# A linear-attention layer with an MLP: another way to spread u, first weights in halves, and other chunks for transposes by DMA

## The chip, the cores and the metric

The kernel runs on one core of a Trainium2 chip. A core has TensorE (PE, matrix products; its weight loads are shown as PEld), VectorE (DVE), ScalarE (ACT), GpSimd (POOL) and SyncE (SP), which here issues nearly all transfers, and 16 DMA engines that carry them. The metric is device time in microseconds, the median of several runs. A profile is one more execution, taken by the hardware profiler.

## What is computed

For each of 4 x 8 heads (batch, head), with 768 steps and width 48, a state of 48 x 48 is carried along; its output of all heads, 384 values a token, goes through an MLP with 2048 hidden values and a leaky ReLU. All inputs are float32.

```python
for t in range(S):
    cur = einsum('bhd,bhe->bhde', u[None] * kt, vt)
    y[:, :, t] = einsum('bhd,bhde->bhe', rt, state + cur)
    state = wt[:, :, :, None] * state + einsum('bhd,bhe->bhde', kt, vt)
x = y.transpose(0, 2, 1, 3).reshape(B * S, H * D)      # 3072 x 384
h = x @ w_in                                           # 3072 x 2048
out = maximum(0.01 * h, h) @ w_out                     # 3072 x 384
```

## The kernel before

The 3072 tokens are 24 chunks of 128 tokens, six for each of the four batch entries. Within a chunk the recurrence is written as matrix products: the logarithm of w is taken (ACT) and summed along time on TensorE (L475, L677), two exponentials of the sums scale r and k (`rk`, L370), `rk` is transposed (`rkT`), scores are formed (L584, L818), masked (`m`, L596, L748) and multiplied with v (`vb`) and with the carried state (`sb`, L612, L619, L784, L789). The term with u is made apart by GpSimd and VectorE: k times u (L400), times r (L404), summed (L408), times v (L412), then added to the output `y`. The output is transposed into `xT`, the MLP's input.

Chunks 0 to 3 are treated as two pairs (`pair`): one load brings 256 tokens, and both chunks go through together. Chunks 4 to 23 go through `single`, each with four loads of 192 KB (w, k, r, v), and `run` forms the scores of one chunk, or of two in one step where the first is in `MERGED`. Each transpose can be done in two ways. On TensorE, `rk` takes eight transposes and two copies out of PSUM (L381, then L386 or L388), an output takes three and one copy (L429, then L434 or L436). By DMA it is one transfer issued by SP (L724 for `rk` of the chunks in `RK_DMA`, L803 for outputs of those in `Y_DMA`).

The MLP runs in blocks of one or two chunks (`blocks`). In a block, 16 parts of the hidden width are formed (up-projection, L860, into `hp`; activation L875 into `g`) and then added up for each chunk in four groups (down-projection, L887), copied out of PSUM (L898, L900) and stored (L904). The weights come in eight loads, four quarters of `w_in` (L313) and four of `w_out` (L318). Each goes through one of ten SBUF buffers of pool `in`, which the loads of chunks use as well, and is cast to bf16 in two halves (L336, L338, L340). An up-projection depends on both casts of the quarter it reads.

Nothing of the order is fixed by the compiler. Every piece of work is a step with a guessed duration for each engine that can do it, a priority, dependences and buffers; class `Plan` runs the steps through an event queue, lets each free engine take the ready step of lowest priority number, and emits the instructions in that order. Each engine works through its own instructions in this order and waits where data are missing. A step with a transfer carries a triple (`wire` time, size, latency). Attention steps of chunk n have priorities around 10 n, the MLP from 1000 on; a store has 5. `AHEAD` keeps the loads of chunk n from being planned before the first sums of chunk n - 8, `LEAD` keeps attention from running more than seven chunks ahead of the MLP. Until `WARM_UNTIL` (24 us of planned time), planned idle time of TensorE is filled with products of zeros (L922), one for each 0.08 us.

u is loaded as one row (L350) and spread over 128 partitions by a float32 product with a column of ones (`ones_f`, L358), then copied to `ub` (L364). The constants at which the planner starts are `BEGIN` (PE 1.1, DVE 3.8 us).

Of the kernel before, what the change touches and what calls it, by code (L numbers as in the profile page):

```python
# [8 lines left out]
F32 = mybir.dt.float32  # L9
# [13 lines left out]
class Plan:  # L23
# [18 lines left out]
    def order(self, pools):  # L42
# [30 lines left out]
        while events:  # L73
# [13 lines left out]
            for e in self.ENGINES:  # L87
# [39 lines left out]
                if wire is None:  # L127
                    self.done[i] = now + d + self.SEEN[e]
                    if self.slack_from <= pri < 1000:
                        self.done[i] += self.slack  # L130
                else:
                    wire, size, lat = wire
# [21 lines left out]

LOAD = (1.05, 64, 1.5)
BOTH = (1.47, 64, 1.6)
WEIGHT = (2.2, 24, 2.6)
STORE = (0.6, 8, 1.5)
ROWS = (0.6, 8, 1.5)
TRK = (1.75, 64, 1.8)  # L160
TY = (0.65, 24, 1.8)


@with_exitstack
def kernel(
# [88 lines left out]
    with tc.manual_schedule():  # L254
# [52 lines left out]

        def weight_steps(q, which, pri):
            st = Buf("in")

            def load(e):
                if which == 0:
                    nc.sync.dma_start(  # L313
                        out=st.t[:].rearrange("p (t f) -> p t f", t=KT),
                        in_=w_in_v[:, :, q * 512 : (q + 1) * 512],
                    )
                else:
                    nc.sync.dma_start(  # L318
                        out=st.t[:].rearrange("p (t f) -> p t f", t=JQ),
                        in_=w_out_v[:, q * JQ : (q + 1) * JQ, :],  # L320
                    )

            ld = step({"SP": 0.5}, load, pri, takes=[st], wire=WEIGHT)
            made = []
            for half in (0, 1):
                def cast(e, half=half):
                    if which == 0:
                        f0 = half * 256
                        o = w_in_b[:, :, q * 512 + f0 : q * 512 + f0 + 256]
                        i = st.t[:].rearrange("p (t f) -> p t f", t=KT)[:, :, f0 : f0 + 256]  # L330
                    else:
                        n = JQ // 2
                        o = w_out_b[:, q * JQ + half * n : q * JQ + (half + 1) * n, :]
                        i = st.t[:].rearrange("p (t f) -> p t f", t=JQ)[:, half * n : (half + 1) * n, :]
                    if e == "POOL":
                        nc.gpsimd.tensor_copy(out=o, in_=i)  # L336
                    elif e == "DVE":
                        nc.vector.tensor_copy(out=o, in_=i)  # L338
                    else:
                        nc.scalar.copy(out=o, in_=i)  # L340
                made.append(step(
                    {"DVE": 1.0 if which == 0 else 0.66, "ACT": 0.83, "POOL": 1.0}, cast, pri + 1, deps=[ld], reads=[st]))
            (win_s if which == 0 else wout_s).append(made)

# [11 lines left out]
        s_u = step(  # L356
            {"PE": 1.4},
            lambda e: nc.tensor.matmul(  # L358
                u_ps.t[:, 0:DM], lhsT=ones_f[:], rhs=u_row.t[0:1, :], start=True, stop=True, skip_group_check=True),
            -20, deps=[u_raw], reads=[u_row], takes=[u_ps])  # L360

# [285 lines left out]
        def single(n):  # L647
# [11 lines left out]
            for i, src in enumerate((w, k, r, v)):  # L659
                def load(e, src=src, i=i):  # L660
                    nc.sync.dma_start(out=part(i)(), in_=src[b, :, t0 : t0 + L, :].rearrange("h p d -> p h d"))
# [56 lines left out]
            if n not in RK_DMA:  # L718
                s_T = [transposes(P0, rk, a, s_d, rkT, lambda a=a: rkT.t[:, a * NP : (a + 1) * NP, :])
                       for a, s_d in ((0, s_r), (1, s_k))]  # L720
            else:
                s_T = [step(
                    {"SP": 0.6},
                    lambda e: nc.sync.dma_start_transpose(  # L724
                        out=rkT.t[:], in_=rk.t[:].rearrange("p a h d -> p (a h d)")),
                    P0, deps=[s_r, s_k], reads=[rk], takes=[rkT], wire=TRK)]
# [71 lines left out]
            if n not in Y_DMA:  # L798
                xt_steps[n] = [to_xt(P0, y, yp, s_ye, lambda: xT[:, :, col : col + L])]
            else:  # L800
                xt_steps[n] = [step(
                    {"SP": 0.6},
                    lambda e: nc.sync.dma_start_transpose(  # L803
                        out=xT[:, :, col : col + L], in_=y.t[:].rearrange("p h d -> p (h d)")),
                    P0 + 1, deps=[s_ye], reads=[y], wire=TY)]

# [23 lines left out]
        for n in range(NCH):  # L830
            for q, which in WEIGHTS_AT.get(n, []):
                weight_steps(q, which, n * 10 - 8)
            if n < done_to:
# [12 lines left out]
        for nb, size in enumerate(blocks):  # L846
# [33 lines left out]
            for ch in chs:  # L880
# [3 lines left out]
                for q in range(4):  # L884
                    def down(e, op=op, g=g, q=q, off=off):
# [70 lines left out]
```

## Time and profile before

| | |
|---|---|
| median of 3 runs | 183.1 us (182.97 to 184.17) |
| profiled execution | 185.71 us, its span 184.0 us |
| granted TensorE clock | 0.999 |
| busy: DVE, ACT, POOL | 114.0, 114.7, 98.9 us |
| DMA: moved, mean rate | 34.48 MB, 187 GB/s |
| DMA: time of packets, share of 16 engines' span | 88.5% |
| transposes by DMA: `xT`, `rkT` | 14 and 11, 3.7 and 4.0 us from issue to landing |
| loads of a chunk | 3.8 to 4.2 us from issue to landing |

Rows of the profile name the line of the kernel, the engine, the operation and the tiles (out <- in), with buffer numbers left out; xN counts instructions. In rows in order of time, the first number is the start and the second the length in microseconds, and a bracket gives the engine's idle time before it and what ended it. Rows with SPq are issues by SP: their length is the issuing, not the transfer. The chain of waits is followed back from the last instruction, at each step to what came last; its rows give start, length, engine and line. Rows by stretch give, behind the stretch and its length, busy time and number of instructions of PE, PEld, DVE, ACT and POOL, then the granted clock, the DMA share and GB/s. Ends of matmuls are modelled, so single matmuls are shown longer than the pace at which they follow one another.

### The profile page before, as it was taken

To read this page: it belongs to the slowest core of one execution; us is meant where nothing else is said; L and a number is where in the kernel's file an instruction comes from. 1 tells how busy PE (TensorE), PEld (TensorE's weight loads), DVE (VectorE), ACT (ScalarE), POOL (GpSimd) and SP (SyncE) were. 2 spreads that over 40 slices of the span, in tenths; PEclk is the share of its full clock that TensorE was granted. 3 is DMA by queue.
4 is the path that set the end of the run, shared out by engine and by line. 5 is a ranking of instruction groups with operands and counts; after the bars stand their busy time and mean duration, and the time that the engine had idled before them with its cause. 6 is when DMAs were issued, how large, how long until landed. Compare 5 with 4: busy or idle time off the path is not lost.

```text
span 184.0 us, 5300 instructions
## 1 busy us (share of the span) xinstructions
PE 176.9 (96%) x2091; PEld 133.8 (73%) x2091; DVE 114.0 (62%) x231; ACT 114.7 (62%) x251; POOL 98.9 (54%) x140
## 2 busy tenths in 40 slices
PE   7999999999999999999998999999999999999991
PEld 5676787777877888777685687776686686777750
DVE  4388864298898769695975487595383486521102
ACT  2566879685886886957384676574566663454510
POOL 6788610665978689764664549546347555000000
PEclk9999999999999999999999999999999999999999
DMA  5999999899997999899799998999699995520112
GB/s 143 261 261 369 382 376 329 155 224 213 185 225 137 212 178 223 147 222 185 134 180 160 216 178 179 219 139 223 146 231 203 167 242 93 121 64 4 43 43 86
DMA packets 116154, 34.48 MB, mean 187 GB/s; under 512 B 109473, under 2 KB 114594, under 8 KB 116130
## 3 DMA queue, kind: packets, MB, share of 16 engines
q1 hardware_dynamic: 116128, 34.16, 88.5%
q8 instruction: 16, 0.26, 0.7%
q14 instruction: 8, 0.07, 0.1%
q10 hardware_dynamic: 2, 0.00, 0.0%
HBM read 25.17 MB, written 4.72 MB: 162 GB/s over the span
## 4 chain that ended last, share of the span: by engine, by line
PE 80%; DMA 9%; DVE 3%; issue 2%; ACT 2%; SPq 1%; POOL 1%; DVEq 0%; ACTq 0%; POOLq 0%
PE ps L860 30%; PE ps L887 28%; DMA in<-in_r_dram 5%; PE ps L922 3%; PE ps L818 3%; PE ps L381 3%; DMA xT<-y 2%; DMA in<-in_v_dram 2%; PE ps L475 2%; PE ps L789 2%; PE ps L677 1%; PE ps L758 1%; PE ps L612 1%; DVE rk L370 1%; PE ps L784 1%
## 5 line engine op out<-in xcount | busy, mean ns | idle before, releaser
L860 PE MATMUL ps<-xT,w_in_b 128*128 128x256 bf16 (+1 forms) x672 | 74.2, 257 | 0.2
L887 PE MATMUL ps<-w_out_b,g 128*128 128x384 bf16 x384 | 73.9, 326 | 0.0
L875 ACT ACTIVATE g<-ps 128x512 bf16<-128x512 f32 x96 | 56.2, 597 | 27.7 <-PE ps L860 26.8
L860 PEld LDWEIGHTS <-w_in_b 128*128 128x128 bf16 x672 | 56.3, 98 | 10.0 <-issue 0.5
L887 PEld LDWEIGHTS <-g 128*128 128x128 bf16 x384 | 35.5, 98 | 17.5
L400 POOL TENSOR_TENSOR ru<-in,ub 128x384 f32<-128x384 f32 x24 | 23.9, 999 | 21.3 <-DMA in<-in_k_dram 18.0
L370 DVE TENSOR_TENSOR rk<-in,ps 128x384 bf16<-128x384 f32 x48 | 24.9, 549 | 13.0 <-DMA in<-in_r_dram 5.0
L748 DVE TENSOR_TENSOR m<-ps,maskb 128x512 bf16<-128x512 f32 x40 | 25.2, 683 | 6.6 <-PE ps L818 6.5
L404 POOL TENSOR_TENSOR ru<-ru,in 128x384 f32<-128x384 f32 x24 | 23.9, 999 | 4.2 <-DMA in<-in_r_dram 3.7
L898 DVE COPY o<-ps 128x384 f32<-128x384 f32 x12 | 6.7, 558 | 19.0 <-PE ps L887 18.8
L412 POOL TENSOR_TENSOR vs<-in,dg 128x384 f32<-128x384 f32 x20 | 16.6, 830 | 3.3 <-DVE dg L408 3.1
L735 POOL TENSOR_TENSOR sb<-s,a 128x384 bf16<-128x384 f32 x18 | 14.9, 829 | 4.4 <-ACT a L698 4.4
L420 POOL CAST vb<-in 128x384 bf16<-128x384 f32 x24 | 12.0, 505 | 9.8 <-DMA in<-in_v_dram 9.0
L689 DVE TENSOR_TENSOR ci<-ps,lw 128x384 f32<-128x384 f32 x20 | 11.1, 556 | 8.0 <-PE ps L680 3.2
L408 DVE TENSOR_REDUCE dg<-ru 128x8 f32<-128x384 f32 x24 | 13.1, 548 | 4.2 <-POOL ru L404 3.9
L671 ACT ACTIVATE lw<-in 128x384 bf16<-128x384 f32 x20 | 10.4, 522 | 5.4 <-DMA in<-in_w_dram 5.3
L443 DVE TENSOR_TENSOR y<-ps,vs 128x384 bf16<-128x384 f32 x20 | 11.1, 553 | 2.7 <-PE ps L789 2.2
L388 ACT COPY rkT<-ps 128x512 bf16<-128x512 bf16 x17 | 9.8, 586 | 3.5 <-PE ps L381 3.3
L698 ACT ACTIVATE a<-ps 64x4 f32<-64x4 f32 x36 | 6.1, 168 | 9.5 <-DVE ci L689 6.4
L703 ACT ACTIVATE ps<-ps 128x384 f32<-128x384 f32 x20 | 9.6, 482 | 2.0 <-DVE ci L689 1.9
L381 PE MATMUL ps<-ident,rk 128*128 128x128 bf16 x104 | 10.0, 223 | 0.2
L707 ACT ACTIVATE ps<-ci 128x384 f32<-128x384 f32 x20 | 9.8, 490 | 0.0
(87 smaller groups left out, 172.8 us busy)
## 6 DMA issues: line engine op xcount, KB each, us to landing
out_dram<-o SPq DMA_DIRECT2D x24, 192.0 KB, 3.1
in<-in_w_dram SPq DMA_DIRECT2D x20, 192.0 KB, 3.8
in<-in_k_dram SPq DMA_DIRECT2D x20, 192.0 KB, 3.9
in<-in_r_dram SPq DMA_DIRECT2D x20, 192.0 KB, 4.2
in<-in_v_dram SPq DMA_DIRECT2D x20, 192.0 KB, 4.1
in<-in_moe_w_in_dram SPq DMA_DIRECT2D x4, 768.0 KB, 9.4
in<-in_moe_w_out_dram SPq DMA_DIRECT2D x4, 768.0 KB, 13.0
in<-in_w_dram SPq DMA_DIRECT2D x2, 384.0 KB, 5.1
```

What stands on the lines that cost most here:

```text
L370: nc.vector.tensor_tensor(out=o, in0=x, in1=i, op=ALU.mult)
L381: nc.tensor.transpose(view()[:, g, :], rk.t[:, kind, 2 * g : 2 * g + 2, :].rearrange("p h d -> p (h d)"), ident[:])
L400: lambda e: nc.gpsimd.tensor_tensor(out=ru.t[:], in0=kv(), in1=ubv, op=ALU.mult),
L404: lambda e: nc.gpsimd.tensor_tensor(out=ru.t[:], in0=ru.t[:], in1=rv(), op=ALU.mult),
L408: lambda e: nc.vector.tensor_reduce(out=dg.t[:], in_=ru.t[:], axis=AX.X, op=ALU.add),
L412: lambda e: nc.gpsimd.tensor_tensor(out=vs.t[:], in0=vv(), in1=dg.t[:].unsqueeze(2).to_broadcast([128, H, D]), op=ALU.mult),
L420: {"POOL": 0.56}, lambda e: nc.gpsimd.tensor_copy(out=vb.t[:], in_=vv()),
L735: lambda e: nc.gpsimd.tensor_tensor(out=sb.t[:].rearrange("p g a d -> p (g a) d"), in0=s_in.t[:].rearrange("p g a d -> p (g a) d"), in1=a_ ...
L748: lambda e, par=par: nc.vector.tensor_tensor(out=m.t[:, par, :, :], in0=sc[par].t[:].rearrange("p (g t) -> p g t", g=NP), in1=maskb[:].uns ...
L860: nc.tensor.matmul(hp.t[:, a * N : (a + 1) * N], lhsT=w_in_b[:, t, (j + a) * 128 : (j + a + 1) * 128], rhs=xT[:, t, c0 : c0 + N], start=(a ...
L875: lambda e, hp=hp, g=g, j=j, J=J, N=N: nc.scalar.activation(out=g.t[:, j : j + J, 0:N], in_=hp.t[:, 0 : J * N].rearrange("p (a n) -> p a n ...
L887: nc.tensor.matmul(op.t[:, 0:DM], lhsT=g.t[:, j, off : off + 128], rhs=w_out_b[:, j, :], start=(j == 0), stop=(j == NJ - 1))
```

## The change

- u: the row is split into three parts by two subtractions on VectorE. `top` views the upper 16 bits of each float32 word as a bf16 number; the part is what is left when it is subtracted. Three bf16 products with a row of ones add the three upper halves in PSUM. `ones_f` becomes bf16.
- Weights: the first two quarters of `w_in` are loaded as four halves, each into a buffer of its own; the rest as before. An up-projection depends only on the casts of the 256 columns that it reads.
- `RK_DMA`: 6 and 16 are added, 18 is taken out. `Y_DMA`: 6, 10, 12, 13 and 16 are taken out. `MERGED`: 6 and 22 are added and 8 is taken out, so 6 and 7, and 22 and 23 share their scores, and 8 and 9 do not.
- `blocks`: chunks 2 and 3 become blocks of one, 6 and 7 become one block.
- `AHEAD` 8 becomes 4, and the planner's times for transfers and for issuing them change. These act through the order of the instructions alone.

```diff
-                    dma_free = max(dma_free, free[e] + 0.2) + wire
+                    dma_free = max(dma_free, free[e] + lead) + wire
...
-LOAD = (1.05, 64, 1.5)
-BOTH = (1.47, 64, 1.6)
-WEIGHT = (2.2, 24, 2.6)
-STORE = (0.6, 8, 1.5)
-ROWS = (0.6, 8, 1.5)
-TRK = (1.75, 64, 1.8)
-TY = (0.65, 24, 1.8)
+LOAD = (1.1, 64, 1.4, 0.2)
+BOTH = (1.5, 64, 1.6, 0.2)
+WEIGHT = (2.06, 24, 2.6, 0.2)
+HALF = (1.06, 16, 2.6, 0.2)
+STORE = (0.45, 8, 0.9, 0.2)
+TRK = (1.7, 64, 0.9, -0.6)
+TY = (0.95, 24, 0.7, -0.6)
...
-    RK_DMA = {10, 12, 14, 15, 17, 18, 19, 20, 21, 22, 23}
-    Y_DMA = {6, 10, 11, 12, 13, 14, 15, 16, 17, 19, 20, 21, 22, 23}
-    MERGED = {8, 10, 12, 14, 16, 18, 20}
+    RK_DMA = {6, 10, 12, 14, 15, 16, 17, 19, 20, 21, 22, 23}
+    Y_DMA = {11, 14, 15, 17, 19, 20, 21, 22, 23}
+    MERGED = {6, 10, 12, 14, 16, 18, 20, 22}
-    AHEAD = 8
+    AHEAD = 4
-    WEIGHTS_AT = {4: [(q, x) for x in (0, 1) for q in range(NQ)]}
-    blocks = [2, 2, 1, 1, 1, 1, 2, 2, 2, 2, 2, 2, 2, 2]
+    WEIGHTS = [(0, x, x + 1, 32) for x in range(4)] + [(x, 2 * q, 2 * q + 2, 32) for x in (0, 1) for q in range(NQ) if 2 * x + q > 1]
+    blocks = [2, 1, 1, 1, 1, 2, 2, 2, 2, 2, 2, 2, 2, 2]
...
-    ones_f = pool.tile([1, 128], F32, name="ones_f")
+    ones_f = pool.tile([1, 128], BF16, name="ones_f")
...
-        def weight_steps(q, which, pri):
+        def weight_steps(which, lo, hi, pri):
             st = Buf("in")
+            n = hi - lo
...
-            ld = step({"SP": 0.5}, load, pri, takes=[st], wire=WEIGHT)
+            ld = step({"SP": 0.6}, load, pri, takes=[st], wire=WEIGHT if n == 2 else HALF)
...
-            fetch_u, -30, takes=[u_row], wire=(0.05, 1, 1.5))
+            fetch_u, -30, takes=[u_row], wire=(0.05, 1, 1.6, 0.2))
...
-        s_u = step(
-            {"PE": 1.4},
-            lambda e: nc.tensor.matmul(
-                u_ps.t[:, 0:DM], lhsT=ones_f[:], rhs=u_row.t[0:1, :], start=True, stop=True, skip_group_check=True),
-            -20, deps=[u_raw], reads=[u_row], takes=[u_ps])
+        u_parts = [Buf("o"), Buf("o")]
+
+        def top(t):
+            return t[0:1, :].bitcast(BF16).rearrange("p (d two) -> p d two", two=2)[:, :, 1]
+
+        before, chain = u_row, [u_raw]
+        for part in u_parts:
+            chain.append(step(
+                {"DVE": 0.5},
+                lambda e, part=part, before=before: nc.vector.tensor_tensor(
+                    out=part.t[0:1, :], in0=before.t[0:1, :], in1=top(before.t), op=ALU.subtract),
+                -20, deps=[chain[-1]], reads=[before], takes=[part]))
+            before = part
+
+        def u_spread(e):
+            for x, t in enumerate([u_row, *u_parts]):
+                nc.tensor.matmul(
+                    u_ps.t[:, 0:DM], lhsT=ones_f[:], rhs=top(t.t), start=(x == 0), stop=(x == 2),
+                    skip_group_check=True)
+        s_u = step({"PE": 0.6}, u_spread, -20, deps=[chain[-1]], reads=[u_row, *u_parts], takes=[u_ps])
...
-                    {"SP": 0.5}, load, P0 + i * 0.1, takes=[slot], wire=LOAD,
+                    {"SP": 0.62}, load, P0 + i * 0.1, takes=[slot], wire=LOAD,
...
-                    {"SP": 0.6},
+                    {"SP": 1.3},
...
-                    deps=[s for ch in chs for s in xt_steps[ch]] + win_s[j * 128 // 512])
+                    deps=[s for ch in chs for s in xt_steps[ch]] + win_s[j // 2 : (j + J) // 2])
...
-                        deps=g_done[q * 4 : q * 4 + 4] + wout_s[q] + [s_dn], reads=[g], takes=[op])
+                        deps=g_done[q * 4 : q * 4 + 4] + wout_s[2 * q : 2 * q + 2] + [s_dn], reads=[g], takes=[op])
...
-                    {"SP": 0.5},
+                    {"SP": 0.6},
```

More of the change, by code (lines that the diff above doesn't have):

```diff
@@ L313, in load @@
                     nc.sync.dma_start(
-                        out=st.t[:].rearrange("p (t f) -> p t f", t=KT),
-                        in_=w_in_v[:, :, q * 512 : (q + 1) * 512],
+                        out=st.t[:, 0 : KT * n * 256].rearrange("p (t f) -> p t f", t=KT),
+                        in_=w_in_v[:, :, lo * 256 : hi * 256],
                     )
@@ L318, in load, with cast @@
                     nc.sync.dma_start(
-                        out=st.t[:].rearrange("p (t f) -> p t f", t=JQ),
-                        in_=w_out_v[:, q * JQ : (q + 1) * JQ, :],
-                    )
-            ld = step({"SP": 0.5}, load, pri, takes=[st], wire=WEIGHT)
-            made = []
-            for half in (0, 1):
-                def cast(e, half=half):
+                        out=st.t[:, 0 : n * 2 * DM].rearrange("p (t f) -> p t f", t=2 * n),
+                        in_=w_out_v[:, lo * 2 : hi * 2, :],
+                    )
+            ld = step({"SP": 0.6}, load, pri, takes=[st], wire=WEIGHT if n == 2 else HALF)
+            for x in range(lo, hi):
+                def cast(e, x=x):
                     if which == 0:
-                        f0 = half * 256
-                        o = w_in_b[:, :, q * 512 + f0 : q * 512 + f0 + 256]
-                        i = st.t[:].rearrange("p (t f) -> p t f", t=KT)[:, :, f0 : f0 + 256]
-                    else:
-                        n = JQ // 2
-                        o = w_out_b[:, q * JQ + half * n : q * JQ + (half + 1) * n, :]
-                        i = st.t[:].rearrange("p (t f) -> p t f", t=JQ)[:, half * n : (half + 1) * n, :]
+                        o = w_in_b[:, :, x * 256 : (x + 1) * 256]
+                        i = st.t[:, 0 : KT * n * 256].rearrange("p (t f) -> p t f", t=KT)[
+                            :, :, (x - lo) * 256 : (x - lo + 1) * 256]
+                    else:
+                        o = w_out_b[:, 2 * x : 2 * x + 2, :]
+                        i = st.t[:, 0 : n * 2 * DM].rearrange("p (t f) -> p t f", t=2 * n)[
+                            :, 2 * (x - lo) : 2 * (x - lo) + 2, :]
                     if e == "POOL":
@@ L340, in cast @@
                         nc.scalar.copy(out=o, in_=i)
[L341 removed]
+                (win_s if which == 0 else wout_s).append(step(
                     {"DVE": 1.0 if which == 0 else 0.66, "ACT": 0.83, "POOL": 1.0}, cast, pri + 1, deps=[ld], reads=[st]))
[L343 removed]
         xt_steps, lns, firsts, rows = {}, {}, {}, {}
@@ L830 @@
         for n in range(NCH):
-            for q, which in WEIGHTS_AT.get(n, []):
-                weight_steps(q, which, n * 10 - 8)
+            if n == B:
+                for which, lo, hi, pri in WEIGHTS:
+                    weight_steps(which, lo, hi, pri)
             if n < done_to:
```

4 lines of the change are left out of this document (2 added, 2 removed).

## Prediction

> **What bounds the kernel now.** I read the page's engine line first, then the chain of waits in order of time, then the order of instructions around its bends, then busy time by stretch.
>
> ```profile
> PE 176.9 (96%) x2091; PEld 133.8 (73%) x2091; DVE 114.0 (62%) x231; ACT 114.7 (62%) x251; POOL 98.9 (54%) x140
> ```
> ```profile
> 1.06 2.53 PE ps L922 x22
> 3.58 1.57 PE ps L358 x2
> 5.16 1.50 PE ps L922 x13
> 6.66 1.92 PE ps L475 x6
> ...
> 20.87 0.56 PE ps L922 x10
> 21.43 1.33 PE ps L860 x12
> ...
> 60.75 5.33 DMA in<-in_r_dram
> ...
> 174.83 5.21 PE ps L887 x32
> ```
>
> TensorE is the bound: of 184.0 us it is idle 184.0 - 176.9 = 7.1, of which 1.06 lie before its first matmul and 3.96 after its last (174.83 + 5.21 = 180.04, to 184.0), so about 2.1 us of visible holes are left. From 21.43 on it does up- and down-projections with attention steps between them. Three things can shorten the run: reaching 21.43 earlier, fewer columns to stream, fewer holes. The end, 32 down matmuls, their copy and store, is in the new program as it was.
>
> The time is formed as a difference. The profiled execution took 185.7 us, a span of 184.0 and 1.7 around it; the median of the three runs is 183.1, 2.6 lower, and I take the same difference off both.
>
> **The change part by part. Spreading u.** L358, two f32 passes, takes 1.57 us of TensorE. In its place stand two subtractions on VectorE and three bf16 products.
>
> ```profile
> 4.75 0.84 ACT L467 ACTIVATE lw<-in 128x768 bf16<-128x768 f32 x1 [2.12 <-DMA in<-in_w_dram]
> 5.20 0.56 DVE L364 COPY ub<-ps 128x384 f32<-128x384 f32 x1 [2.29 <-PE ps L358]
> 6.37 1.95 POOL L400 TENSOR_TENSOR ru<-in,ub 128x384 f32<-128x384 f32 x2 [0.99 <-DMA in<-in_k_dram]
> 7.84 0.55 DVE L370 TENSOR_TENSOR rk<-in,ps 128x384 bf16<-128x384 f32 x1 [2.09 <-ACT ps L505]
> 11.11 0.67 PE L922 MATMUL ps<-zeros 128*128 128x128 bf16 x9
> ```
>
> u itself is not awaited: its copy ends at 5.76, and its first user L400 sits until 6.37 for k. The subtractions cost nothing as long as VectorE idles (2.29 us before 5.20, 2.09 before 7.84); two at 0.55 are 1.1, and 1.1 would be their price without that cover. What counts is when L475 runs. Its input is ready at 4.75 + 0.84 = 5.59, and it starts at 6.66, behind 13 fillers: 1.07 us late. The number of fillers comes from the planner's constants: it now places the products at 3.8 + 2 x 0.55 = 4.9, so it emits (4.9 - 1.1 - 0.1) / 0.08 = 46 fillers before them and none after. A filler takes 1.50 / 13 = 0.115 us early and 0.56 / 10 = 0.056 later; L475 takes 1.92 / 6 = 0.32 each, so 0.16 at the later rate. The rate changes when TensorE has worked without L358 in between for 3.4 us (5.16 to 8.58 was still slow) to 5.9 us (by 11.11 nine fillers take 0.67, or 0.074 each). From 1.06, unbroken, that is 4.5 to 7.0.
> If at 4.5: 30 slow fillers and 16 fast ones end at 5.4, the products (3 x 0.16) at 5.9, the six L475 at 6.85 instead of 8.58: a gain of 1.7. If at 7.0: 46 slow fillers end at 6.35, the products at about 7.15, and the first two L475, for which ScalarE waits, at 7.47 instead of 7.30: a loss of 0.2. I take the middle, 0.75 gained.
> The Trainium skill has a rule for this ("TensorE: Matmul & The Clock Gate", Part 1): the array runs at half its clock until one free-running window of some 3.4 us has been busy throughout, so the turn varies from run to run. This trace agrees as far as it goes (3.42 us of slow work from 5.16 to 8.58), and an unbroken filler from 1.06 would by the rule turn between 4.5 and 7.9, which leaves the middle about where it is and makes the loss a little more likely.
>
> **First weights in halves.** Up-projection of the first two chunks needs xT of both and a cast quarter of w_in.
>
> ```profile
> 19.83 1.63 POOL L336 CAST w_in_b<-in 128x768 bf16<-128x768 f32 x2
> 20.01 0.48 ACT L436 COPY xT<-ps 128x384 bf16<-128x384 bf16 x1 [0.17 <-PE ps L429]
> 20.38 0.84 ACT L340 CAST w_in_b<-in 128x768 bf16<-128x768 f32 x1
> ```
> ```profile
> 10.39 3.29 SPq L313 DMA_DIRECT2D in<-in_moe_w_in_dram  x4
> 13.73 9.20 SPq L318 DMA_DIRECT2D in<-in_moe_w_out_dram  x4
> ```
>
> xT is there at 20.49, the first cast half at 19.83 + 0.82 = 20.65, the second half at 21.22; the first up starts behind the latter. Each half now is awaited by itself, so the first up can start about 21.22 - 20.65 = 0.57 sooner (0 if the planner puts the cast elsewhere); that the half lands sooner lets its cast follow when xT moves. I take 0.55. Two more issues at 3.29 / 4 = 0.82 us stand ahead of w_out on SP's queue; they cost nothing, since SP spends 9.20 - 4 x 0.82 = 5.9 us waiting there for buffers, and 1.6 without that cover.
> Against this part the Trainium skill says ("DMA: Bandwidth & Descriptors", Rules for kernel authors) to join small transfers into one, and its fixed share is about 2 us for each. An estimate by that page, with no cover, is two more transfers at 2 us, 4 us of loading before w_out; no run here shows such an uncovered share, and I keep nothing for it.
>
> **Transposes moved.** Outputs of chunks 6, 10, 12, 13 and 16 go back from DMA to TensorE; rk of 6 and 16 goes to DMA, rk of 18 comes back; one more pair of chunks shares its scores.
>
> ```profile
> 27.11 0.33 PE ps L429 x6
> ...
> 38.05 0.22 PE ps L381 x4
> ...
> 40.13 0.33 PE ps L818 x8
> ...
> 78.44 0.55 PE ps L818 x16
> ```
>
> Outputs: 5 x 0.33 / 2 = +0.83. rk: one set fewer, 2 x 0.22 = -0.44. Scores: 0.55 for two against 2 x 0.33, -0.11. TensorE gets about +0.3 us. Copies to SBUF change by +5 x 0.48 and about -2 x 0.6, 1.2 us on engines busy 62%: hidden, 1.2 at most. Other block sizes stream the same columns.
>
> **Holes.** By stretch, and around the largest one:
>
> ```profile
> 94.00:100.00 6.00, 5.24 (x55) 4.12 (x54) 3.60 (x7) 4.10 (x9) 3.53 (x5) 1.00 1.17 176
> 100.00:106.00 6.00, 5.82 (x59) 3.79 (x59) 2.79 (x6) 3.48 (x9) 3.60 (x5) 1.00 0.93 187
> ```
> ```profile
> 99.48 0.52 ACT L671 ACTIVATE lw<-in 128x384 bf16<-128x384 f32 x1 [1.10 <-DMA in<-in_w_dram]
> 100.06 0.32 PE L677 MATMUL ps<-lw,trev 128*128 128x384 bf16 x1 [0.81 <-ACT lw L671]
> ...
> 72.07 3.02 SPq L724 DMA_TRANSPOSE rkT<-rk  x1
> 84.63 1.46 SPq L803 DMA_TRANSPOSE xT<-y  x1
> 93.17 2.39 SPq L724 DMA_TRANSPOSE rkT<-rk  x1
> 95.61 0.57 SPq L661 DMA_DIRECT2D in<-in_w_dram  x1
> 96.90 2.89 SPq L803 DMA_TRANSPOSE xT<-y  x2
> 118.80 2.92 SPq L724 DMA_TRANSPOSE rkT<-rk  x1
> ```
>
> 0.76 + 0.18 = 0.94 us of the 2.1 lie in these twelve. SP issues in order: a transpose at its head that waits for its data holds the loads behind it, w, r and v of later chunks. The pair at 96.90 is chunks 12 and 13, the transpose at 84.63 is chunk 10, that at 118.80 (the sixth of rk) is chunk 18: all three leave SP. The one right ahead of the late w, at 93.17, is chunk 14 and stays; what stood before it gets shorter by the 1.46 at 84.63. New at its head are chunks 6 and 16, at up to 3.02 each like the one at 72.07. Also, load order: AHEAD 4 instead of 8 lets a load be planned only four chunks ahead; the loads shown land just in time anyway, so I price it at nothing, between the bounds of this part: 2.1 gained (no hole left) and 3.5 lost (the first rival). Nearest are the 0.94 just shown, for which two holders of three go: I take 0.9 gained, the row's own size, and half of it would not surprise.
>
> Sum: -0.75 - 0.55 + 0.3 - 0.9 = -1.9. That gives 183.8 in a profile and 183.1 - 1.9 = **181.2** as median.
>
> **Rivals. A new hole at chunks 6 and 7 (slower).** They become one block with shared scores, and 6 waits for DMA.
>
> ```profile
> 51.30 0.40 PE L818 MATMUL ps<-rkT 48*128 48x128 bf16 x8
> 56.27 0.40 PE L818 MATMUL ps<-rkT 48*128 48x128 bf16 x8
> 61.34 0.83 PE L860 MATMUL ps<-xT,w_in_b 128*128 128x128 bf16 x12
> 62.01 0.81 PE L887 MATMUL ps<-w_out_b,g 128*128 128x384 bf16 x4
> 66.28 0.62 PE L818 MATMUL ps<-rkT 48*128 48x128 bf16 x16
> 71.63 0.34 PE L429 MATMUL ps<-ident,y 128*128 128x128 bf16 x3
> 73.12 0.33 PE L429 MATMUL ps<-ident,y 128*128 128x128 bf16 x3
> ```
>
> Now the scores of 6 (51.30) and 7 (56.27) stand apart, and TensorE takes up chunk 6 alone at 61.34. Shared, they wait for 7; the pair at 66.28 needed 5.35 and 6.84 us to its output transposes, so 6 and 7 come to 61.6 and 63.1, with the copy 63.9 at the latest. TensorE, 1.3 earlier, wants them at 60.0 and has about two older down groups (like that at 62.01) of 4 x 5.21 / 32 = 0.65 left: a hole of 63.9 - 60.0 - 1.3 = 2.6. The loads behind 6's transpose on SP cost once more what they cost at 94 to 106, 0.94. 183.1 - 1.3 + 0.3 + 2.6 + 0.9 = 185.6. For it: VectorE and the loads set the pace of attention there. Against: attention of chunks 8 and 9 can fill the hole. It decides when the first up of 6 and 7 comes after about 63.
> **The start gives nothing.** Either the filler stays slow (-0.2) or TensorE, earlier, meets loads that come no earlier: the chain passes a load of 5.33 us at 60.75. 183.1 + 0.3 - 0.9 = 182.5.
> **All of it.** The turn at 4.5 and every hole gone: 183.1 - 1.7 - 0.55 + 0.3 - 2.1 = 179.0.
>
> **How the numbers follow.** Forecast 0.44 (180.4 to 182.0, two thirds of it below 181.3), all of it 0.14, no start 0.23, new hole 0.19. One per cent, 1.8 us, is what a measurement tells from no change: faster 0.30 + 0.14 = 0.44, same 0.14 + 0.23 + 0.02 = 0.39, slower 0.17. The range leaves out the slow end and a little at the fast one: 179.2 to 184.9.
>
> **What would show it.** Start: L475 near 6 us, the first L860 between 19.9 and 20.3; at 21 or later the term is wrong. Moves: 45 transposes of outputs on TensorE instead of 30 (L429), 96 of rk instead of 104 (L381). Holes: TensorE's idle time without its ends falls from 2.1 towards 1.2; the 94 to 106 stretch is full. Slower: idle time on L860 around 60 to 64, or releasers from rkT's DMA on TensorE. The forecast is wrong if TensorE's work, not its holes or its start, makes the difference.

## The result, and the profile after

The changed kernel takes 182.61 us (median of 11 runs, 181.91 to 183.08); the kernel before, run beside it on the same chip, 184.02 us (11 runs, 182.97 to 185.28). The ratio is 0.9925, interval 0.9899 to 0.9951: faster by about 1.4 us. The forecast was 181.2 on a base of 183.1, a difference of 1.9. Later, on two chips, the same changed kernel gave 0.9901 [0.987, 0.9932] and 0.9889 [0.9842, 0.9935]. Ratios leave out executions that took over 1.5 per cent more than the fastest of their kernel.

The page's engine line of the changed kernel, and, from the groups by line, the two kinds of transposes on TensorE (line, engine, tiles, shapes, count, then busy time and mean of one in ns):

```profile
PE 174.7 (96%) x2102; PEld 134.4 (74%) x2102; DVE 116.1 (64%) x235; ACT 113.9 (63%) x251; POOL 100.5 (55%) x141
```
```profile
L395 PE MATMUL ps<-ident,rk 128*128 128x128 bf16 x96 | 8.4, 220 | 0.2 <-DVE rk L384 0.2
L443 PE MATMUL ps<-ident,y 128*128 128x128 bf16 x45 | 5.0, 219 | 0.3 <-DVE y L651 0.3
```

TensorE is still the bound, and the counts are those forecast, 96 and 45. Lines have moved: L358 is now L371, L381 L395, L400 L414, L429 L443, L475 L489, L860 L875, L887 L902. The span went from 184.0 to 181.2. The chain of waits in order of time (start, length) shows the start anew:

```profile
1.32 4.60 DMA in<-in_k_dram
6.14 1.44 issue
7.62 1.96 POOL ru L414 x2
9.57 1.91 POOL ru L418 x2
11.49 0.91 POOL vb L434 x2
...
14.93 1.06 PE ps L626 x54
15.99 0.79 issue
20.69 0.83 PE ps L875 x6
...
172.30 5.21 PE ps L902 x32
```

Before, the chain up to 20 us ran over TensorE and the first up-projection stood at 21.43 (21.27 in the timeline). Now it passes through GpSimd's product with u (L414), and the first up comes at 20.69. The timeline says why GpSimd entered; the fence of one row is from before, for the start of the sums:

```profile
1.06 5.09 PE L937 MATMUL ps<-zeros 128*128 128x128 bf16 x46 [1.06 <-DVE zeros L255]
6.08 0.86 PE L371 MATMUL ps<-o,ones_f 1*128 1x384 bf16 x3
6.87 0.34 PE L489 MATMUL ps<-lw,tstr 128*128 128x384 bf16 x1
6.97 0.56 DVE L378 COPY ub<-ps 128x384 f32<-128x384 f32 x1 [3.02 <-PE ps L371]
7.62 1.00 POOL L414 TENSOR_TENSOR ru<-in,ub 128x384 f32<-128x384 f32 x1 [1.48 <-DVE ub L378]
```
```profile
6.45 0.53 PE L475 MATMUL ps<-lw,tstr 128*128 128x384 bf16 x1
```

All 46 fillers now precede u's products; they took 5.09 us. u is spread at 7.53 instead of 5.76, and GpSimd waits 1.48 us for it. The first sums start at 6.87 instead of 6.45 (6.66 in the chain), at the faster rate. The second chunk's xT is ready at 20.06 + 0.48 = 20.54 (next fence), before at 20.49: the new way of spreading u brought the first block nothing in this execution. A pause of TensorE near 16 us, told in the last section, took 0.79 us here and 0.45 in the profile before, so 0.34 of that is the pause. The first up then starts behind the cast of a half instead of the second half of a quarter:

```profile
19.69 0.94 DVE L338 CAST w_in_b<-in 128x768 bf16<-128x768 f32 x1
...
20.06 0.48 ACT L450 COPY xT<-ps 128x384 bf16<-128x384 bf16 x1 [0.17 <-PE ps L443]
```

In the middle the stretch from 94 to 106, where the forecast had 0.94 us of holes, is full (columns: length, then busy time and count of PE, PEld, DVE, ACT, POOL, granted clock, DMA share, GB/s), and TensorE shows no row with an idle time from 60 us to the end of its work:

```profile
94.00:106.00 12.00, 11.96 (x123) 9.35 (x122) 7.30 (x15) 9.92 (x24) 8.84 (x11) 1.00 1.18 207
```

### The profile page after: what moved, and what is told of

Read it like the earlier page. It is cut to its first block, busy times and chain, and to the rows that moved or that the text cites. A ratio compares the mean times of both kernels' runs of the same rounds, so it can differ in the third digit from the quotient of the medians.

```text
span 181.2 us, 5321 instructions
## 1 busy us (share of the span) xinstructions
PE 174.7 (96%) x2102; PEld 134.4 (74%) x2102; DVE 116.1 (64%) x235; ACT 113.9 (63%) x251; POOL 100.5 (55%) x141
## 4 chain that ended last, share of the span: by engine, by line
PE 90%; POOL 3%; DMA 3%; issue 1%; DVE 1%; ACT 0%; SPq 0%; DVEq 0%; POOLq 0%
PE ps L875 35%; PE ps L902 35%; PE ps L832 3%; PE ps L395 3%; DMA in<-in_k_dram 3%; PE ps L803 2%; PE ps L691 2%; PE ps L443 2%; PE ps L798 2%; PE ps L772 2%; PE ps L626 1%; POOL ru L414 1%; POOL ru L418 1%; PE ps L694 1%; PE ps L489 1%
## 5 line engine op out<-in xcount | busy, mean ns | idle before, releaser
L875 PE MATMUL ps<-xT,w_in_b 128*128 128x256 bf16 (+1 forms) x672 | 74.6, 257 | 0.0
L902 PE MATMUL ps<-w_out_b,g 128*128 128x384 bf16 x384 | 72.5, 326 | 0.0
L875 PEld LDWEIGHTS <-w_in_b 128*128 128x128 bf16 x672 | 56.4, 98 | 9.5 <-DVE w_in_b L338 0.2
L902 PEld LDWEIGHTS <-g 128*128 128x128 bf16 x384 | 35.5, 98 | 18.0
L414 POOL TENSOR_TENSOR ru<-in,ub 128x384 f32<-128x384 f32 x24 | 23.9, 1001 | 15.9 <-DMA in<-in_k_dram 11.2
L913 DVE COPY o<-ps 128x384 f32<-128x384 f32 x11 | 6.1, 557 | 19.8 <-PE ps L902 19.5
L787 DVE TENSOR_TENSOR s<-ps,sb 128x384 f32<-128x384 f32 x14 | 7.8, 555 | 4.7 <-PE ps L772 4.6
L402 ACT COPY rkT<-ps 128x512 bf16<-128x512 bf16 x15 | 8.6, 588 | 3.3 <-PE ps L395 3.0
L937 PE MATMUL ps<-zeros 128*128 128x128 bf16 x80 | 9.0, 274 | 1.1 <-DVE zeros L255 1.1
```

The source lines that it names most:

```text
L414: lambda e: nc.gpsimd.tensor_tensor(out=ru.t[:], in0=kv(), in1=ubv, op=ALU.mult),
L875: nc.tensor.matmul(hp.t[:, a * N : (a + 1) * N], lhsT=w_in_b[:, t, (j + a) * 128 : (j + a + 1) * 128], rhs=xT[:, t, c0 : c0 + N], start=(a ...
L902: nc.tensor.matmul(op.t[:, 0:DM], lhsT=g.t[:, j, off : off + 128], rhs=w_out_b[:, j, :], start=(j == 0), stop=(j == NJ - 1))
```

## The experiments

The chips of the calls differ (before took 183.8 to 185.75), so kernels are compared by their ratio to the kernel before on the same chip. The table gathers the profiles: start of the first up (timeline), of the last group of down matmuls (chain), the time between, and the holes behind 21 us, or behind the first up where that is later. The holes are my own sum over TensorE's rows in order of time: from the end of one row, less the 0.16 us by which modelled ends overlap, to the next row's start, where that is over 0.05; they are good to some 0.1 us. With new sets in before, the last group counts 36 matmuls instead of 32 and so starts 0.65 us earlier than the others' would.

| kernel | ratio to before | first up | last group | between | holes |
|---|---|---|---|---|---|
| before (the profile shown) | 1 | 21.27 | 174.83 | 153.6 | 5.5 |
| before again | 1.0012 [0.9983, 1.0041] | 20.97 | 172.61 | 151.6 | 3.7 |
| changed (the profile shown) | 0.9925 [0.9899, 0.9951] | 20.69 | 172.30 | 151.6 | 3.4 |
| changed, second | 0.9901 [0.987, 0.9932] | 19.11 | 171.83 | 152.7 | 4.3 |
| changed, third | 0.9889 [0.9842, 0.9935] | 20.41 | 173.62 | 153.2 | 5.0 |
| changed, u by the old product | 0.9914 [0.9886, 0.9942] | 20.12 | 171.01 | 150.9 | 2.6 |
| changed, products earlier | 0.9926 [0.9902, 0.9949] | 19.80 | 171.11 | 151.3 | 3.0 |
| changed, whole quarters | 0.9883 [0.981, 0.9956] | 20.24 | 171.56 | 151.3 | 3.2 |
| changed, whole quarters, second | 0.99 [0.9851, 0.9949] | 20.02 | 172.10 | 152.1 | 3.9 |
| changed, old u and whole quarters | 0.9923 [0.9888, 0.9958] | 20.81 | 171.75 | 150.9 | 2.9 |
| changed, first up 1.0 us late | 0.989 [0.9848, 0.9931] | 20.02 | 171.54 | 151.5 | 3.5 |
| changed, first up 3.0 us late | 0.9975 [0.9945, 1.0006] | 23.74 | 175.02 | 151.3 | 3.2 |
| changed, old sets | 1.0053 [1.0009, 1.0097] | 19.38 | 175.34 | 156.0 | 7.9 |
| before, new sets | 1.0046 [1.0017, 1.0074] | 20.96 | 172.74 | 151.8 | 4.4 |
| before, new planner times | 1.014 [1.0063, 1.0216] | 22.70 | 174.87 | 152.2 | 4.1 |
| before, halves | 1.0052 [1.0019, 1.0086] | 20.30 | 174.32 | 154.0 | 6.2 |
| changed, nudged | 0.9949 [0.9911, 0.9988] | 19.13 | 172.64 | 153.5 | 4.9 |
| before, nudged | 0.9984 [0.9942, 1.0025] | 20.71 | 172.88 | 152.2 | 4.4 |
| before, new sets and times | 0.9964 [0.9924, 1.0003] | 24.17 | 177.15 | 153.0 | 4.7 |
| before, new sets and times, second | none formed | 24.12 | 174.85 | 150.7 | 2.5 |

One profile against another says little below 1 us: the same kernel's holes range over 1.6 to 1.8 us. The verdicts go by the ratios.

**Was the first profile of before an ordinary one?** The kernel before, unchanged.

> The kernel before, unchanged, profiled a second time. Theory S (the profile that the prediction was made from was a slow execution, and part of its holes were that execution's): span 182.0 to 182.7, TensorE idle between its first and last matmul at most 1.4 us instead of 2.1, the hole of 0.81 us near 100 us gone or moved. Rival (the profile was typical, the new one simply gains less in the middle): span 183.7 to 184.3 and the hole again at 94 to 106 us. Ratio 1.00 in both.

Median 183.80 us, and the stretch in question was full in this profile:

```profile
94.00:106.00 12.00, 11.93 (x127) 8.94 (x123) 7.84 (x16) 7.88 (x18) 5.57 (x8) 1.00 0.98 180
```

The hole near 100 us, on which the forecast sized its last term, belonged to that one execution of 185.71 us, 1.7 above the 184.0 that 11 runs gave.

**u by the old product**, in the changed kernel's order, with as many fillers before and behind it as the kernel before has:

```diff
-                lambda e, part=part, before=before: nc.vector.tensor_tensor(
-                    out=part.t[0:1, :], in0=before.t[0:1, :], in1=top(before.t), op=ALU.subtract),
+                lambda e: None,
...
-            for x, t in enumerate([u_row, *u_parts]):
-                nc.tensor.matmul(
-                    u_ps.t[:, 0:DM], lhsT=ones_f[:], rhs=top(t.t), start=(x == 0), stop=(x == 2),
-                    skip_group_check=True)
+            nc.tensor.matmul(
+                u_ps.t[:, 0:DM], lhsT=ones_f[:], rhs=u_row.t[0:1, :], start=True, stop=True, skip_group_check=True)
```

> The changed kernel in its own order, but u spread as before: 22 fillers, the f32 product, 13 fillers, no subtractions. Theory U (the new spreading gives nothing: TensorE's rate still turns only near 6 us and u is now awaited by GpSimd): ratio within 0.15% of the changed kernel's 0.9925, first up-projection within 0.2 us of 20.69. Rival R (the spreading carries 0.75 us as predicted): ratio 0.9965, first up near 21.4.

0.9914 [0.9886, 0.9942], against 0.9925 of the change: at the end no gain of the three bf16 products shows.

**The products earlier**, 26 fillers ahead of them and three behind, so that GpSimd gets u sooner:

```diff
+                    if i == s_u:
+                        count = 26
+                    if after_u:
+                        count, after_u = 3, False
```

> The changed kernel in its own order, with 26 fillers ahead of the three products and 3 behind them, in place of 46 and none. Theory G (46 fillers hold u until 7.5 us, GpSimd's products with u start 1.25 us late, and the chain of waits of the first 20 us hangs on them): L414 starts near 6.2 instead of 7.62, the second chunk's xT is 0.5 to 1.2 us earlier, the time 0.4 to 1.0 us lower than the changed kernel's. Rival C (the sums run at half rate then, and eat it up): xT within 0.2 us of 20.54, time within 0.3 us.

The first up came at 19.80, 0.9 earlier than in the first profile of the change, though later than in its second (19.11); the time did not move: 0.9926 [0.9902, 0.9949].

**The sets alone**, in the kernel before, with its planner times:

```diff
-    RK_DMA = {10, 12, 14, 15, 17, 18, 19, 20, 21, 22, 23}
-    Y_DMA = {6, 10, 11, 12, 13, 14, 15, 16, 17, 19, 20, 21, 22, 23}
-    MERGED = {8, 10, 12, 14, 16, 18, 20}
+    RK_DMA = {6, 10, 12, 14, 15, 16, 17, 19, 20, 21, 22, 23}
+    Y_DMA = {11, 14, 15, 17, 19, 20, 21, 22, 23}
+    MERGED = {6, 10, 12, 14, 16, 18, 20, 22}
...
-    blocks = [2, 2, 1, 1, 1, 1, 2, 2, 2, 2, 2, 2, 2, 2]
+    blocks = [2, 1, 1, 1, 1, 2, 2, 2, 2, 2, 2, 2, 2, 2]
```

> The kernel before with the changed sets for transposes, shared scores and block sizes alone; old u, whole quarters, old planner times. Theory M (the moved transposes carry the gain of the middle): ratio 0.994 to 0.997, span about 0.7 us under that of before. Rival P (the planner's times and load order carry it, the sets fit only with them): ratio 1.000 or above.

1.0046 [1.0017, 1.0074], no gain. **The changed kernel with the old sets** is the same edit the other way round:

> The changed kernel with the old sets for transposes, shared scores and blocks. Theory M (the moved transposes, with planner times that fit, carry the gain of the middle): ratio 0.997 or above, 0.8 us or more over the changed kernel. Theory H (only the first weights in halves carry it): the same as the changed kernel within 0.4 us.

1.0053 [1.0009, 1.0097]: without the new sets the rest of the change loses all of its gain. Its TensorE timeline shows where (in brackets the idle time and what ended it):

```profile
65.00 0.32 PE L691 MATMUL ps<-lw,trev 128*128 128x384 bf16 x1 [1.26 <-ACT lw L685]
...
131.72 2.14 PE L875 MATMUL ps<-xT,w_in_b 128*128 128x256 bf16 x18 [0.92 <-DMA xT<-y]
157.21 0.40 PE L832 MATMUL ps<-rkT 48*128 48x128 bf16 x8 [1.07 <-DMA rkT<-rk]
```

This execution was the slowest of its ten, 186.34 us, so the sizes are on the high side. Two of the three waits end with the landing of a transpose by DMA. The new planner times take such a transpose as landed about 1 us sooner (`rkT` 1.3 - 0.6 + 1.7 + 0.9 = 3.3 us behind the start of its issue instead of 0.6 + 0.2 + 1.75 + 1.8 = 4.35, with nothing ahead of it), so the order leaves its users less room. Fewer outputs on DMA would leave fewer such places; that fits, and was not tried transpose by transpose.

**The changed kernel again**, nothing edited, on the chip of the run just told and of the following two:

> The changed kernel, unchanged, beside the others of this call. Its ratio on record is 0.9925. Theory U (the new spreading of u is a loss inside the change) expects it 0.3 to 0.8 us slower than the kernel with the old u in the new order was (181.85 us, 0.9914); rival N (that difference is scatter between calls) expects a median within 0.3 us of 181.9.

Here the fillers took 4.30 us instead of 5.09, u was spread at 6.57, and the first up started at 19.11, 1.58 earlier than in the first profile. The last group started only 0.47 earlier; the holes had grown by 0.9, one of them in the stretch that was full before:

```profile
97.59 0.33 PE L772 MATMUL ps<-vb,rk 128*128 128x96 bf16 x4 [0.60 <-POOL vb L434]
```

**The planner times alone**, with `AHEAD` 4, in the kernel before:

```diff
-LOAD = (1.05, 64, 1.5)
+LOAD = (1.1, 64, 1.4, 0.2)
...
-TRK = (1.75, 64, 1.8)
-TY = (0.65, 24, 1.8)
+TRK = (1.7, 64, 0.9, -0.6)
+TY = (0.95, 24, 0.7, -0.6)
...
-    AHEAD = 8
+    AHEAD = 4
```

> The kernel before with the new planner times and AHEAD 4 alone. Theory P (the order that comes from them carries the gain): ratio 0.993 to 0.996. Theories H and M: 0.998 to 1.003, first up-projection at 21.1 to 21.4 as before.

1.014 [1.0063, 1.0216], slower than any theory had it. Its first up stands at 22.70, 1.7 later than in the second profile of before; the last section returns to why. **The halves alone**, in the kernel before, with the loads, casts and dependences as changed:

```diff
-    WEIGHTS_AT = {4: [(q, x) for x in (0, 1) for q in range(NQ)]}
+    WEIGHTS = [(0, x, x + 1, 32) for x in range(4)] + [(x, 2 * q, 2 * q + 2, 32) for x in (0, 1) for q in range(NQ) if 2 * x + q > 1]
...
-                    deps=[s for ch in chs for s in xt_steps[ch]] + win_s[j * 128 // 512])
+                    deps=[s for ch in chs for s in xt_steps[ch]] + win_s[j // 2 : (j + J) // 2])
```

> The kernel before with the first weight quarters in halves, and up-projections waiting only for the casts of their own columns, alone. Theory H (the start is what the change gains, and it reaches the end): first up 0.5 to 1.0 us earlier than 21.1, ratio 0.994 to 0.997. Rival A (an earlier start is taken back by loads that come no earlier): first up earlier, ratio 0.999 to 1.002.

The first up came 0.7 earlier than in the second profile of before, about what was forecast, and the kernel was slower, 1.0052 [1.0019, 1.0086]. The order behind it had other holes in its profile, such as these:

```profile
97.50 0.32 PE L677 MATMUL ps<-lw,trev 128*128 128x384 bf16 x1 [0.45 <-ACT lw L671]
...
120.92 0.32 PE L677 MATMUL ps<-lw,trev 128*128 128x384 bf16 x1 [0.59 <-ACT lw L671]
158.42 0.40 PE L818 MATMUL ps<-rkT 48*128 48x128 bf16 x8 [0.53 <-DMA rkT<-rk]
```

**How far do small nudges of an order move the time?** The planner's wire time of a load, in the changed kernel and in the one before:

```diff
-LOAD = (1.1, 64, 1.4, 0.2)
+LOAD = (1.12, 64, 1.4, 0.2)
```

> The changed kernel with one planner time moved by 2% (LOAD 1.1 becomes 1.12): same work, another order. Theory L (what the change gains is one order that happens to leave few holes on TensorE; any other order loses it): ratio 0.997 or above, holes on TensorE 1 us or more above the changed kernel's. Theory C (sets, planner times and halves together give good orders, this one too): ratio 0.988 to 0.995.

```diff
-LOAD = (1.05, 64, 1.5)
+LOAD = (1.07, 64, 1.5)
```

> The kernel before with LOAD 1.05 moved to 1.07: same work, another order. Theory L: ratio 1.003 or above, since the order of before was a good one too. Rival (before's order is an ordinary one): 0.997 to 1.003.

0.9949 [0.9911, 0.9988] and 0.9984 [0.9942, 1.0025]. Seven of the ten executions of the nudged change took 183.18 to 184.21 us, and the ratio is theirs; the other three took 186.04 to 186.07. The order of before is an ordinary one. The changed order may lose half of its gain by a nudge of 2 per cent; the interval reaches from little lost to nearly all.

**The first up 1.0 us later**, by 18 more fillers ahead of it in the changed kernel:

```diff
-                    for _ in range(max(0, int((s - pe_free - 0.1) / 0.08))):
+                    for _ in range(max(0, int((s - pe_free - 0.1) / 0.08)) + (18 if i == up_first[0] else 0)):
```

> The changed kernel in its own order with 18 more fillers, 1.0 us of TensorE, ahead of the first up-projection. Theory E (TensorE is the bound from there on, so what is gained at the start reaches the end): 1.0 us slower than the changed kernel, ratio 0.996 to 0.998. Theory A (the start is taken back by waits for loads further on): less than 0.4 us slower, ratio 0.990 to 0.994.

0.989 [0.9848, 0.9931], no worse than the change without them: no cost of the delay shows. The change itself was not run on this chip; 1.0 us is 0.005 of the time, and the end of the interval leaves room for about half of it. **Whole quarters in the changed kernel**, on the same chip:

```diff
-    WEIGHTS = [(0, x, x + 1, 32) for x in range(4)] + [(x, 2 * q, 2 * q + 2, 32) for x in (0, 1) for q in range(NQ) if 2 * x + q > 1]
+    WEIGHTS = [(x, 2 * q, 2 * q + 2, 32) for x in (0, 1) for q in range(NQ)]
```

> The changed kernel with the first weights in whole quarters again (up-projections still wait only for the casts of their own columns). Theory H (halves bring the first up forward): first up 0.5 to 0.8 us later than with halves at the same rate of TensorE, and 0.2 to 0.8 us slower. Theory L: up or down by up to 1% with its own order, whatever the first up does.

0.9883 [0.981, 0.9956]; no gain of the halves shows at the end either. **Sets and planner times together**, in the kernel before (the edits of both above):

> The kernel before with the new sets, block sizes and planner times together; u as before, whole quarters as before, up-projections waiting for both casts as before. Theory J (the gain is that of sets and times together, in the middle; the start gives nothing): ratio 0.987 to 0.994, with a first up-projection no earlier than 21. Rival (the start is needed for it): 0.996 or above.

0.9964 [0.9924, 1.0003], between the theories. Its executions fall apart by the granted clock: three of the twelve kept 0.999 or more and took 183.51, 183.60 and 185.22 us; nine had 0.986 to 0.991 and took 185.50 to 187.81 (before: 185.75). On the same chip **the first up 3.0 us later** (54 in place of 18), **the changed kernel a third time** and **whole quarters again**:

> The changed kernel in its own order with 54 more fillers, 3.0 us of TensorE, ahead of the first up-projection. If there is slack of about 1 us behind the start, as 18 fillers suggest: 1.5 to 2.5 us slower than the changed kernel of this call. If the start has no weight at all: less than 0.7 us slower. If 18 fillers were hidden by scatter and TensorE is the bound: 3.0 us slower.

> The changed kernel, unchanged, as the reference of this call: ratio 0.989 to 0.993. Its 46 fillers take between 4.0 and 5.1 us by where the clock turns, and the first up starts between 19.0 and 20.7 with it.

> The changed kernel with whole quarters, again, beside the changed kernel: theory J expects the two within 0.5 us of each other; theory H expects the changed kernel 0.4 to 0.8 us faster.

185.53 us with 3.0 us more, against 184.07 without and 183.79 with whole quarters. Of 3.0 us about half, 1.46, reached the end; some 1.5 us of slack lie between the first up and the end. The profiles agree: first up 3.33 later than in the third profile, last group 1.40 later.

**Both parts of the start undone at once**, in the changed kernel (the edits of the old product and of whole quarters), and sets and times again beside it:

> The changed kernel with both changes of its start undone at once: one float32 product for u (22 fillers ahead, 13 behind) and whole quarters of w_in; sets, block sizes and planner times as changed. Theory M (the gain lies in the order of the middle, which sets and planner times make together; each part of the start is worth nothing, and both together too): ratio 0.988 to 0.994 to the kernel before. Rival B (the two parts of the start cover for each other, so that one of them is needed): 0.995 to 1.000.

> The kernel before with the changed sets, block sizes and planner times, as once already, on the same chip as the kernel that has both parts of the start undone. The two differ in how the planner places u's product and its copy, and so in the fillers and in the order that follows. Theory M: the same ratio as that kernel within 0.3 per cent. Rival O (one planned order differs from the next by some 0.5 per cent, whatever the parts): above it by 0.3 per cent or more, at 0.995 to 0.999, as before.

The first gave 182.57 us and 0.9923 [0.9888, 0.9958]: as fast as the whole change. Its start is that of before, row by row up to the sums (up-projections still wait only for the casts that they read):

```profile
1.06 2.53 PE ps L943 x22
3.59 1.57 PE ps L369 x2
5.16 1.50 PE ps L943 x13
6.66 1.92 PE ps L486 x6
...
20.81 1.48 PE ps L872 x12
```

The second did not settle: five of its six times lie from 184.17 to 186.64, one at 181.35, so no ratio is formed (before: 184.06). Four of the six had a clock of 0.986 to 0.991 (185.40 us and more); the others took 181.35 and 184.17. It has the same sets and planner times as the first, but its first up came at 24.12, in the earlier profile at 24.17, over 3 us late; the last section returns to why. That is the same size of delay as the 3.0 us put in on purpose, and 0.9964 is about the 0.9975 that those cost. That the delay is all that parts the two kernels fits, but was not tried by taking it away.

## Where the prediction was wrong, and where right

The step that failed is in "reaching 21.43 earlier": the sum counts what the start gains, 0.75 + 0.55 = 1.3 us, one for one as time at the end. With both parts of the start undone the kernel keeps the whole gain (0.9923). The middle, counted at 0.6, brings 1.4 instead. That -1.9 came out 0.5 from the measured difference is luck: one term too large by 1.3, another too small by 0.8.

**Base.** 183.1 was the median of three runs; eleven runs beside the change gave 184.02. As a ratio the forecast was 181.2 / 183.1 = 0.9896, inside the intervals of the second and third measurement of the change, and 0.0003 outside that of the first. The number itself lies 1.4 us under the measured 182.61: 0.9 of it is the base, 0.5 the difference.

**Start, spreading u (-0.75): wrong.** "u itself is not awaited" held only for the old place. Behind 46 fillers u came at 7.53 in the first profile of the change, 1.77 us later, and at 6.57 in the second; GpSimd waited 1.48 and 0.52 us for it. The bracket for the turn of the rate was too late at its early end. By the prediction's count a turn at 4.5 ends the fillers 4.34 us behind their start (5.4 - 1.06); of nine profiles with 46 unbroken fillers four were quicker (3.98, 4.16, 4.29 and 4.30), and five took 4.94 to 5.09. By the same rates the quickest turned at about 3.8, an estimate from these numbers, or 2.7 us behind the first filler. The rule cited with it (the Trainium skill, "TensorE: Matmul & The Clock Gate", Part 1) has the turn vary between runs, and these nine agree; its 3.4 us of busy work before the turn the quickest does not bear out.

**Start, halves (-0.55): right in place, wrong in worth.** In the kernel with halves alone the first up came 0.7 earlier (20.30 against 20.97), and the same with the old product in the changed kernel (20.12 against 20.81 with whole quarters); at the end whole quarters cost nothing that shows. Nor does a cost of the two added transfers: 184.07 with them, 183.79 without. The 4 us of the estimate by the Trainium skill ("DMA: Bandwidth & Descriptors", Anatomy of one DMA — SWDGE (gpsimd) path) show in no run here. That page fits its 2 us a transfer for transfers issued by GpSimd, whereas SP issues these.

**The step behind both** is thus the count one for one. A delay of 1.0 us and the undoing of both parts change nothing that shows, and a delay of 3.0 costs 1.5. Had the 1.3 us reached the end, undoing both parts would have given 0.996 to 0.9996 (the three ratios of the change, and 0.0071 more), above the interval measured, 0.9888 to 0.9958. So the rival that "the start gives nothing" had that half right. Its reason, that an earlier TensorE meets attention steps that come no earlier, fits: in the second profile of the change the first up came 1.58 earlier and the holes were 0.9 larger. Which loads or engines pace these steps was not tried by itself.

**Columns (+0.3): right.** Counts as forecast. The time between first up and last group less the holes was 148.1 (21.27 to 174.83, less 5.5) and 148.0 in before, 148.2 and 148.4 in the first two profiles of the change.

**Holes (-0.9): the middle gains, and more, but the evidence was wrong.** With the start as before, sets and planner times gain 1.4 us (0.9923 of 184.06, interval 0.8 to 2.1), where the forecast had -0.9 + 0.3 = -0.6 for them. The hole that gave the size was not there in the next execution. That the gain lies in holes is argued: with the start undone they come to 2.9, in before to 5.5 and 3.7, a difference about as large as the scatter. The sign that the prediction named did not come. TensorE's idle time without its ends is 181.2 - 174.7 - 1.06 - 3.69 = 1.75 in the first profile of the change (0.79 of it the pause near 16 us); in the second profile of before, by the same count, it is 0.8. Neither half brings the gain: the sets alone 1.0046, the times with old sets 1.0053. `AHEAD`, priced at nothing, does nothing here: with 8 in its place the changed planner puts out the same program.

**Rivals.** The new hole at chunks 6 and 7 did not come: no matmul of the change shows an idle time from 60 us on. "All of it" did not come either. "The start gives nothing" is nearest in mechanism; its 182.5 meets 182.61 by luck, since on its base of 183.1 it allows 0.6, and the middle gave 1.4.

**Covers.** The two subtractions run from 2.84 to 3.96, where VectorE idled before, and VectorE's idle time before u's copy still grew from 2.29 to 3.02: they are hidden.

**Open.** How much of the gain belongs to these sets and times as such, and how much to one lucky order that they produce: the nudge by 2 per cent leaves 0.9949, between both.

## What to carry to other kernels

Before sizing a hole, set the profiled execution's time against the runs, and look whether a second execution has the hole; a base of three runs was off by half a per cent here. Reaching the steady part earlier counts only as far as nothing behind it paces the work: put a delay there first and see whether it costs anything. Constants of a planner and the choices made under them (here sets for DMA, and when it believes a transpose landed) belong together; tested one by one, each looked like a loss (the times alone met the pause told below besides).

## What the runs showed of the hardware

**TensorE stops near 16 us, waiting for nothing that the profile shows.** In 12 of the 20 profiles its stream pauses, with a bracket "issue": nine times for 0.19 to 0.79 us, and three times for 1.70 to 2.19. It is always behind the 222nd or 223rd matmul on record, whatever the order. In the changed kernel, and in the second run of sets and times:

```profile
14.86 1.13 PE L626 MATMUL ps<-vb,m 64*64 64x48 bf16 x54
16.78 0.34 PE L626 MATMUL ps<-vb,m 64*64 64x48 bf16 x10 [0.79 <-issue]
```
```profile
16.27 0.32 PE L619 MATMUL ps<-sb,rkT 128*64 128x96 bf16 x3
18.78 0.56 PE L619 MATMUL ps<-sb,rkT 128*64 128x96 bf16 x5 [2.19 <-issue]
```

In the latter the granted clock (the third number from the right) fell behind the pause, and came back; in each half us from 18.5 to 21.5 it was 0.50:

```profile
18.00:24.00 6.00, 5.22 (x87) 4.32 (x87) 3.11 (x7) 3.35 (x6) 0.98 (x2) 0.72 1.05 384
24.00:30.00 6.00, 6.00 (x121) 5.25 (x119) 4.44 (x7) 4.32 (x8) 3.09 (x4) 1.00 1.07 375
```

The first profile of sets and times shows the same, with a pause of 1.92 us. Pause and half clock together are of the size of the 3 us by which sets and times, put into the kernel before, start late. Planner times alone pause 1.70 us at the same place without a fall of the clock, and start 1.7 us late. What precedes the pause is one packet of a DMA queue for instructions. The view of DMA queues for 16.2 to 16.5 us of the second run of sets and times (queue, packets, MB, share):

```profile
q1 hardware_dynamic: 61, 0.11, 97.2%
q8 instruction: 1, 0.02, 23.5%
```

In every profile one such packet shows between 12.3 and 16.5 us, and where TensorE pauses, it resumes 2.6 to 3.1 us behind the start of the stretch of 0.3 us that holds it; the eight that do not pause reach the place 2.8 to 3.2 us behind it. With 3.0 us of fillers more, TensorE pauses a second time, at 22.73, for 0.48 us, 2.6 us behind the next such packet and 128 matmuls behind the first pause. The data queue takes about all of the DMA engines at the time. That the packet is TensorE's own code, held up behind loads, fits: the queue moves 16 packets in all for 4204 matmuls and weight loads, 263 a packet, and 128 matmuls with their weight loads are 256. It was only argued, not tried. The Trainium skill ("Runtime: NRT & Kernel Launch", Instruction fetch mechanics) has code arrive in blocks of 16 KiB, at a cost that it calls mostly hidden; the 0.19 to 2.19 us here were not hidden from TensorE, though the slack behind the start, some 1.5 us, can hide the shorter ones from the time.

**The filler's rate turns at another time in each execution.** Forty-six fillers from 1.06 on took between 3.98 us (in the nudged change) and 5.09. The granted clock is shown as 1.00 from 1.0 to 7.0 us in the nine profiles that have them, so the turn shows in the fillers' own pace alone.
